# Float64 weight words converted without a clamp, and another written order of the first half of a fused attention and two-MLP kernel

## Chip, cores and metric

The kernel runs on one core of one Trainium2 chip. The metric is the device time of one execution in microseconds (us). A core has TensorE (PE, with its weight loads listed as PEld), VectorE (DVE), ScalarE (ACT), GpSimd (POOL) and SyncE (SP), which here issues all transfers.

## What is computed

Windowed attention with a few global tokens, then two MLPs one after the other. Activations are float32; the weights reach the kernel as float64 words.

```python
# attention: batch 4, heads 8, 512 local and 32 global tokens, head size 64, window 32
s_g  = scale * q_g @ [k_g, k_l].T ;  out_g = sm(s_g) @ [v_g, v_l]
s_l  = [scale * q_l @ k_g.T, where(|i - j| <= 32, scale * q_l @ k_l.T, -1e9)]
out_l = sm(s_l) @ [v_g, v_l]
x = concat(out_g, out_l)                      # 2176 tokens x 512
# first MLP, 512 -> 1024 -> 512
h = x @ w_in ; solu = h * softmax(h)
x = layernorm(solu) * g_ln @ w_out
# second MLP, 512 -> 2048 -> 512
h = x @ w_in2
g = where(h >= 1, h, where(h <= -1, 0, (h + 1) ** 2 / 4))
out = g @ w_out2
```

## The kernel before

Tokens go in 17 tiles of 128. A float32 product is made of three reduced-precision products (high x high, high x low, low x high), so each matrix needs a high and a low part. `conv` makes these from a piece of weights, 128x512 float64 words, which lie in memory as pairs of 32-bit words (`w.low`, `w.high`). Its steps have letters: A takes the magnitude of the high word, C clamps it, B shifts it left by 3, D puts the sign in, F puts in three bits of the low word, m scales by the layernorm gain (second matrix only), H rounds to the high part, L subtracts to get the low part. B, D and F run on VectorE; A and H on ScalarE or VectorE; C and L on GpSimd or VectorE.

The first half of the kernel is written out by hand in `SCRIPT`, a list of tokens that `issue` turns into instructions in that order, on every engine's queue at once. A token is a kind and a number; a trailing `v` picks the other engine for that step. Tokens of the attention of tile n: `q`, `v` load; `S` scores, `M` mask, `R` row maximum (negative), `Rn` scale it, `E` exponentials, `T` transposes, `P` copies of them to SBUF (`PT`), `V` product with the values, `I` reciprocal of the sum, `X` normalize, `XT` transpose back. `G` and `Gc` are the scores of the global tokens and their copy. Of the first MLP: `w` loads a piece, `xh`, `xl` split x, `ha`, `hA`, `hb`, `hB` multiply by `w_in` (each half: high part of x, then low part), `mx` row maximum of h, `ex` exponential, `u` the product h * e * (1/sum), `bn`, `pw`, `nn` layernorm, `t`, `th`, `tl` transpose and split, `y` the second product. `Z` is three products of a zero tile that keep TensorE running.

`psA` (3 banks), `psH` (2 pairs of banks) and `psY` hold products. `psH` is shared: the scores `S` of a tile and the products `h` of a tile take turns in it, so a product waits until the reader of the pair two turns earlier is done. Eight pieces of `w_in` (w0 to w7) must be converted before tile 0's products are complete: w0 to w3 for `ha0`, w4 to w7 for `hb0`.

Behind the script come the remaining tiles (`b1`, `b3`, `b4`, `attention` in the order of `ORDER_1`), and then the second MLP, where a loop over 30 half tiles converts one piece per one or two rounds, clamp included, behind the other work of VectorE (line 177 is the clamp, 175 and 174 are step A, 179 B, 181 D, 183 F, 191 L).

Of the kernel before, what the change touches and what calls it, by code (L numbers as in the profile page):

```python
# [53 lines left out]
F2 H2 Ta0 H1v w3 A3v C3 L1 M1 R1 Rn1 Ea1 Z0 q2 S2 G2 Gc2 Eb1 B3 D3 w0 Pa0 A0v C0 M2 R2 Rn2 Ie0v
Ea2 Z0 q3 S3 B0 F3 H3 L3 G3 Z0 Gc3 D0 Tb0 v0 Pb0 V0 w6 q4 w5 M3 Eb2 F0 L2 H0 qg1 gm0 R3 Rn3v gn0
I0 X0 XT0 A6 C6 B6 D6 Ta1 Pa1 Tb1 Pb1 A5v C5 L0 S4 M4 R4 ge0 B5 gt0 gp0 G4 Gc4 Ie1v I1 Ta2 D5 F5
Ie2 F6 H6v L6 Ea3 Eb3 gc0 v1 q5 H5v L5 xh0 xl0 Rn4v V1 Pa2 Tb2 S5 Ie3v X1 XT1 M5 v2 G5 Gc5v R5
I3 w4 A4v C4 w7 Pb2 V2 I2 X2 A7v Ea4 Eb4 Rn5v XT2 q6 Ta3 Tb3 Pa3 Pb3 B4 C7 B7 S6 G6 Gc6v Ea5 Eb5
Ta4 D7 F7 H7 Tb4 v3 V3 ha0 w10 hA0 Ie4v L7 D4 F4 M6 R6 xh1 H4 Pa4 Pb4 X3 L4 XT3 A10 C10 v4 B10
D10 Rn6v Ie5v Ea6 hb0 hB0 mx0 q7 Eb6 G7 Gc7v V4 I4 X4 S7 Ta5 w11 ex0 ze0 z0 u0 w8 A8 C8 M7 R7  # L60
Rn7 B8 Tb5 Pa5 Pb5 w9 Ta6 Tb6 xl1 ha1 hb1 n0 hB1 Ie6v XT4 w14 xh2 xl2 hA1 bn0v pw0 D8 gi0 F8 F10
v5 V5 I5 Ea7 Eb7 A14 mx1 m8 nn0v ex1 ze1v Pa6 Pb6 ha2 hA2 C14v B14 D14 m10 H10 L10 hb2 gm1 ta0
gn1 ge1 q8 hB2 F14 m14 tha0 vn0 gv0 X5 xh3 xl3 z1 qg2 tb0 u1 XT5 tla0 mx2 go0 w13 thb0v tlb0 H14
v6 H8v A9 C9 ex2 ze2 z2 u2 gt1 gp1 gc1 bn1v pw1 nn1v v7 S8 M8 V6 G8 Gc8 I6 X6 L8 B9 q9 ha3 A11
hA3 tb1 thb1 Tb7 Ie7 D9 F9 m9 L14 ta1 w15 hb3 tlb1 tha1v tla1 H9v R8 Ta7 Pa7v L9 v8 Pb7 bn2v hB3
s0 mx3 A13 C13 Rn8v Ea8 Eb8 qg3 G9 C11v B13 B11 Gc9v pw2 nn2v D11 ya0 F11 XT6 I7 m11 V7 X7 H11v
vn1 A15 C15 B15 ex3 ze3v xh4 z3 S9 M9 u3 R9 L11 Rn9 ta2 tha2v tla2 xh5 xl4 tb2 thb2 tlb2 w12 A12
C12 B12 D12 F12 bn3v pw3 Ya0 yca0 Ta8 Pa8v Ea9 Eb9 m12v xl5 ha4 hA4 Tb8 H12 hb4 hB4 mx4 ex4 ze4v
Ie8 gi1 ha5 hA5 z4 u4 nn3v v9 Pb8 D15 F15 D13 F13 L12 hb5 xh6 q10 G10 Gc10 m13 XT7 S10 M10 Ie9
I9 q11 G11 V8 Gc11 H13 L13 hB5 mx5 tb3 m15 gm2 xh7v H15v L15 bn4v yb0 Yb0 ycb0 pw4 ta3 v10 I8 X8  # L70
R10 Rn10 XT8 nn4v A16v C16 thb3v tlb3 Ea10 gv1 tha3v tla3 s1 A17 s2 A18v go1 C17v Tb9 Eb10 Ie10v
B17 ya1 C18v ta4 tha4 tla4 Ta9 Pa9 Pb9 gn2 ex5 ze5 Ya1 yca1 z5 u5 bn5v pw5 ge2 B16 D16 Ta10 tb4
thb4v tlb4 nn5v V9 X9 q12 ha6 S11 M11 R11 F16 XT9 Pa10 xl7 Rn11 Ea11 xl6 hb6 Tb10 xd0 hB6 hA6
mx6 Pb10v D17 F17 I10 ex6 ze6 z6 Eb11 Ie11v yb1 Yb1 ycb1 B18 u6 xd1 D18 F18 H18 L18 ta5 tha5
tla5 S12 H17v M12 bn6v pw6 xh8v xl8 gt2 v11 gp2 R12 Rn12v ha7 hb7 nn6 q13 tb5 thb5v G12 gc2
# [1207 lines left out]
```

## Time and profile before

| | before |
|---|---|
| time, median of 3 runs | 672.46 us (672.03 to 673.53) |
| the profiled execution: its time | 674.86 us |
| its span, first to last instruction | 672.9 us |
| granted TensorE clock, mean | 0.995 |
| busy: PE, DVE, ACT, POOL | 655.8, 432.7, 371.9, 265.0 us |

The span covers the program's own instructions; the time of the execution is 1.96 us longer. Busy time is an average over stages with different limits, so the rows further down are read by stretch.

### The profile page before, as it was taken

To read this page: it belongs to the slowest core of one execution; us is meant where nothing else is said; L and a number is where in the kernel's file an instruction comes from. 1 tells how busy PE (TensorE), PEld (TensorE's weight loads), DVE (VectorE), ACT (ScalarE), POOL (GpSimd) and SP (SyncE) were. 2 spreads that over 40 slices of the span, in tenths; PEclk is the share of its full clock that TensorE was granted. 3 is DMA by queue.
4 is the path that set the end of the run, shared out by engine and by line. 5 is a ranking of instruction groups with operands and counts; after the bars stand their busy time and mean duration, and the time that the engine had idled before them with its cause. 6 is when DMAs were issued, how large, how long until landed. Compare 5 with 4: busy or idle time off the path is not lost.

```text
span 672.9 us, 15123 instructions
## 1 busy us (share of the span) xinstructions
PE 655.8 (97%) x6088; PEld 576.1 (86%) x6092; DVE 432.7 (64%) x766; ACT 371.9 (55%) x917; POOL 265.0 (39%) x298
## 2 busy tenths in 40 slices
PE   7789999999999999999999999999999999999997
PEld 4467888889899889999999998998888888988986
DVE  5898998785777579754887679455555453333332
ACT  5788886766554244435666555554445466444443
POOL 3354543131112114203444676356766655222321
PEclk9899999999999999999999999999999999999999
DMA  8999654319353604301666342653333465734512
GB/s 337 401 353 362 259 183 174 111 49 334 127 193 102 245 31 125 95 1 32 187 188 188 126 126 63 226 212 126 126 126 127 139 204 194 239 131 157 183 67 80
DMA packets 29686, 113.19 MB, mean 168 GB/s; under 512 B 3376, under 2 KB 3888, under 8 KB 27056
## 3 DMA queue, kind: packets, MB, share of 16 engines
q1 hardware_dynamic: 29616, 112.23, 48.0%
q8 instruction: 48, 0.79, 0.5%
q14 instruction: 22, 0.18, 0.1%
HBM read 87.83 MB, written 24.38 MB: 167 GB/s over the span
## 4 chain that ended last, share of the span: by engine, by line
PE 91%; DVE 5%; issue 1%; ACT 1%; DMA 1%; POOL 0%; DVEq 0%; ACTq 0%; POOLq 0%
PE acc L271 27%; PE h L271 25%; PE h L530 14%; PE yT L271 14%; PE plnT L595 2%; PE o L433 2%; PE S L352 2%; PE pPT L418 2%; PE y L271 1%; DVE nm L141 1%; DVE S L141 1%; PE og L493 1%; DVE xy L141 1%; DVE w L181 1%; PE G L405 1%
## 5 line engine op out<-in xcount | busy, mean ns | idle before, releaser
L271 PE MATMUL acc<-wo,g 128*128 128x512 f32 x816 | 211.3, 393 | 0.0
L271 PEld LDWEIGHTS acc<-wo,g 128*128 128x128 f32 x816 | 149.8, 188 | 23.2
L165 POOL TENSOR_TENSOR g<-xy,g 128x384 fp32r<-128x384 f32 (+1 forms) x65 | 62.8, 973 | 139.9 <-ACT g L150 122.4
L150 ACT ACTIVATE xy<-xy 128x384 f32<-128x384 f32 (+1 forms) x144 | 72.7, 505 | 71.9 <-DVE xy L141 68.8
L530 PE MATMUL h<-win,x 128*128 128x512 f32 x408 | 101.4, 400 | 0.9 <-issue 0.9
L271 PE MATMUL yT<-lnT,wout 128*128 128x256 f32 x768 | 95.2, 283 | 0.0
L271 PEld LDWEIGHTS yT<-lnT,wout 128*128 128x128 f32 x768 | 92.8, 189 | 0.8 <-issue 0.2
L530 PEld LDWEIGHTS h<-win,x 128*128 128x128 f32 x408 | 74.8, 188 | 18.1 <-issue 1.7
L141 DVE TENSOR_TENSOR xy<-h,xy 128x384 f32<-128x384 f32 (+1 forms) x64 | 33.5, 524 | 62.4 <-PE h L271 61.0
L778 POOL TENSOR_TENSOR g<-xy,g 128x192 fp32r<-128x192 f32 x60 | 51.4, 876 | 54.2 <-ACT g L150 46.9
L150 ACT ACTIVATE g<-xy 128x384 fp32r<-128x384 f32 (+1 forms) x96 | 48.0, 500 | 18.7 <-DVE xy L141 16.7
L271 PE MATMUL h<-yT,w2i 128*128 128x384 f32 (+1 forms) x300 | 56.4, 334 | 0.0
L150 ACT ACTIVATE xy<-h 128x384 f32<-128x384 f32 (+1 forms) x64 | 30.0, 468 | 45.9 <-PE h L271 45.9
L271 PE MATMUL h<-yT,S 128*128 128x384 f32 (+1 forms) x288 | 54.8, 325 | 0.0
L271 PEld LDWEIGHTS h<-yT,w2i 128*128 128x128 f32 x300 | 52.5, 188 | 2.3
L141 DVE SCALAR_TENSOR_TENSOR xy<-h,xy 128x384 f32<-128x384 f32 (+1 forms) x48 | 26.2, 545 | 43.8 <-ACT xy L150 43.7
L271 PEld LDWEIGHTS h<-yT,S 128*128 128x128 f32 x288 | 48.8, 188 | 5.6 <-DVE xy L141 1.8
L150 ACT ACTIVATE e<-S,nm 128x128 f32<-128x128 f32 x128 | 45.0, 378 | 8.4 <-DVE nm L141 5.7
L518 POOL TENSOR_TENSOR x<-xy,x 128x512 fp32r<-128x512 f32 x17 | 21.8, 1288 | 41.1 <-ACT x L150 41.0
L572 POOL TENSOR_TENSOR rstd<-rstd,nhalf 128x1 f32<-128x1 f32 x17 | 10.3, 603 | 62.7 <-DVE rstd L141 45.5
L271 PE MATMUL h<-yT,lnT 128*128 128x384 f32 (+1 forms) x180 | 34.1, 334 | 0.1
L141 DVE SCALAR_TENSOR_TENSOR xy<-xy 128x384 f32<-128x384 f32 (+1 forms) x48 | 29.0, 603 | 7.5 <-ACT xy L150 7.3
(145 smaller groups left out, 1059.4 us busy)
## 6 DMA issues: line engine op xcount, KB each, us to landing
vw<-in_vwin_dram SPq DMA_DIRECT2D x16, 1024.0 KB, 5.7
wo<-w2d_o SPq DMA_DIRECT2D x32, 512.0 KB, 3.6
qkT<-in_qk_dram SPq DMA_DIRECT2D x15, 768.0 KB, 7.1
wraw<-in_w2i_dram SPq DMA_DIRECT2D x16, 512.0 KB, 4.9
wraw<-in_w2o_dram SPq DMA_DIRECT2D x16, 512.0 KB, 4.3
w2d_o<-wo SPq DMA_DIRECT2D x16, 512.0 KB, 5.2
...
```

The lines of the kernel that those rows point to most:

```text
L141: self.last = getattr(nc.vector, name)(*args, **kw)
L150: vec.act = nc.scalar.activation(**kw)
L165: eng.tensor_tensor(out=lo, in0=src, in1=hi.bitcast(F32), op=ALU.subtract)
L271: mm(out=dst, lhsT=pairs[i][0][x], rhs=pairs[i][1][y], start=start and j == 0, stop=stop and j == 3 * n - 1, **kw)
L352: mm(out=S[32 * hp:32 * hp + 32, par, ci], lhsT=qT[r, hp, ci], rhs=kT[r, hp, w:w + 4].rearrange("p c d -> p (c d)"), start=True, stop=True)
L418: nc.tensor.transpose(ps[:, hp], eT[t][:, HP * par + hp], ident)
L433: mm(out=o[rows, ci, par], lhsT=PT[t][:, par, ci, rows], rhs=w[:, ci, D * h:D * h + D], start=True, stop=True)
L518: eng.tensor_tensor(out=xT[t][1], in0=x[:, :, n:n + P], in1=xT[t][0].bitcast(F32), op=ALU.subtract)
L530: mm(out=hps[t][:, half], lhsT=x[i][:, k], rhs=win[j][:, k, sl], start=not lo and j == 0 and k == 0, stop=lo and k == KD - 1)
L572: nc.gpsimd.tensor_tensor(sts[t].rstd, sts[t].rstd, nhalf, ALU.pow)
L595: nc.tensor.transpose(ps[:, k], ln[t][:, P * c:P * c + P], ident)
L778: eng.tensor_tensor(out=out, in0=x, in1=y, op=ALU.subtract)
```

## The change

The clamp (step C, 19 tokens in the script, and once per piece in the two loops behind it) is gone. Step A is now a product of the high word, read as a float32, with 2^-112: it brings the exponent into float32's place after the shift, and the shift by 3 drops what lay above. B is a shift alone; D takes the sign bit alone. Step A stays on ScalarE (a copy with a scale in place of an absolute value) or, with `v`, on VectorE (a product in place of a bitwise and). C's tokens leave `SCRIPT`, and the whole list stands in another order, with other `v` marks: of the low parts L, six are now on VectorE (before none); of the splits `xh`, seven of nine (before two); of the layernorm's last step `nn`, five of eight (before one).

```diff
 SCRIPT = """
-w1 Z0 A1 C1 B1 D1 Z0 F1 q0 Z0 S0 qg0 G0 Gc0 Z0 w2 Z0 A2 M0 C2 q1 S1 R0 Rn0v Ea0 Eb0 B2 G1 Gc1 D2
+q0 S0 qg0 Z0 M0 R0 Rn0 G0 Gc0v Z0 w0 A0 Ea0 Eb0 B0 D0 F0 H0v q1 S1 M1 R1 G1 L0 Gc1 w2 A2 B2 D2
...
-WORD_LO = 2.0 ** -15
-WORD_HI = 2.0 ** 17 - 2.0 ** -7
+REBIAS = 2.0 ** -112
+SIGN = -1 << 31
...
-            if eng is nc.vector:
-                return nc.vector.tensor_scalar(w.t, w.high, 0x7FFFFFFF, None, ALU.bitwise_and)
-            return nc.scalar.activation(out=w.tf, in_=w.high.bitcast(F32), func=AF.Abs)
-        if step == "C":
-            return clamp.tensor_scalar(w.tf, w.tf, WORD_HI, WORD_LO, ALU.min, ALU.max)
+            if eng is not None:
+                return eng.tensor_scalar(w.tf, w.high.bitcast(F32), REBIAS, None, ALU.mult)
+            return nc.scalar.activation(out=w.tf, in_=w.high.bitcast(F32), func=AF.Copy, scale=REBIAS)
         if step == "B":
-            return nc.vector.tensor_scalar(w.t, w.t, 3, 0x3FFFFFF8, ALU.logical_shift_left, ALU.bitwise_and)
+            return nc.vector.tensor_scalar(w.t, w.t, 3, None, ALU.logical_shift_left)
         if step == "D":
-            return nc.vector.scalar_tensor_tensor(out=w.t, in0=w.high, scalar=-0x40000000, in1=w.t, op0=ALU.bitwise_and, op1=ALU.bitwise_or)
+            return nc.vector.scalar_tensor_tensor(out=w.t, in0=w.high, scalar=SIGN, in1=w.t, op0=ALU.bitwise_and, op1=ALU.bitwise_or)
...
                 if piece_now:
-                    conv("C", piece_now)
+                    conv("B", piece_now)
...
                 if piece_now:
-                    for step in "BDF":
+                    for step in "DF":
                         conv(step, piece_now)
```

The start of VectorE's queue, before (`w_151` is the piece w1, `w_232` is w2; `S` the scores of a tile, `nm` its row maximum):

```order
L179 TENSOR_SCALAR w_151<-w_151 128x512
L181 SCALAR_TENSOR_TENSOR w_151<-xy_89,w_151 128x512
L183 SCALAR_TENSOR_TENSOR w_151<-xy_89,w_151 128x512
L141 TENSOR_TENSOR S<-S,masks 128x8x2x32
L141 MEMSET S 128x2x32
L141 TENSOR_REDUCE nm<-S 128x8
L179 TENSOR_SCALAR w_232<-w_232 128x512
L181 SCALAR_TENSOR_TENSOR w_232<-xy_89,w_232 128x512
L183 SCALAR_TENSOR_TENSOR w_232<-xy_89,w_232 128x512
```

The same place now (`w_218` is the piece w0; `Sg<-G` copies the global scores):

```order
L140 TENSOR_TENSOR S<-S,masks 128x8x2x32
L140 MEMSET S 128x2x32
L140 TENSOR_REDUCE nm<-S 128x8
L140 TENSOR_SCALAR nm<-nm 128x8
L140 COPY Sg<-G 128x160 x2
L176 TENSOR_SCALAR w_218<-w_218 128x512
L178 SCALAR_TENSOR_TENSOR w_218<-xy_89,w_218 128x512
L180 SCALAR_TENSOR_TENSOR w_218<-xy_89,w_218 128x512
L184 CAST win_133<-w_218 128x512
```

The queue now begins with the mask of tile 0 and no longer with a piece. In both orders seven score tiles and nine shifts stand ahead of the first row maximum over h. VectorE's rows up to that maximum otherwise differ by these: now one more D or F (18 for 17), two copies of `PT` (0), one split of x (1 for 0), one reciprocal (5 for 4) and one sum with epsilon (2 for 1), and two steps A fewer (3 for 5). From there to the third maximum over h come further ones: one D or F more, two splits of x, one low part of `wout`, one cast of `wout`, and five small ones, against two copies of `G` fewer.

TensorE's queue where the first products by `w_in` begin (`win_133` is the high part of `w_in`, `win_134` the low), before:

```order
L352 MATMUL S<-qkT 32x128 x32
L405 MATMUL G<-qkT,qkg 32x128 x8
L418 MATMUL pPT<-ident,e 128x128 x8
L433 MATMUL o<-vw,PT 32x64 x32
L530 MATMUL h<-win_133,x 128x512 x4
L530 MATMUL h<-win_134,x 128x512 x4
L530 MATMUL h<-win_133,x 128x512 x8
```

and now:

```order
L415 MATMUL pPT<-ident,e 128x128 x8
L349 MATMUL S<-qkT 32x128 x32
L430 MATMUL o<-vw,PT 32x64 x32
L527 MATMUL h<-win_133,x 128x512 x4
L527 MATMUL h<-win_134,x 128x512 x4
L402 MATMUL G<-qkT,qkg 32x128 x8
L527 MATMUL h<-win_133,x 128x512 x8
```

The same work stands ahead of `ha0` in both (the scores of tiles 0 to 6, the transposes of 0 to 4, the value products of 0 to 3); the scores `G7` now lie inside tile 0's products, before they came behind them.

ScalarE's queue behind the first row maximum over h (`e_1085`, now `e_1046`, is tile 0's exponential and layernorm; `e,rs<-S` are the exponentials of tile 7's scores; `e_1218`, now `e_1280`, is tile 1's), before:

```order
L150 ACTIVATE junk,rstd<-e_1085,nmu 128x1024
L150 ACTIVATE rstd<-rstd 128x1
L150 ACTIVATE e,rs<-S,nm 128x128 x8
L175 ACTIVATE w_1211<-wraw 128x512
L150 ACTIVATE nmu<-nmu,rstd 128x1
L150 ACTIVATE e_1085<-e_1085,nmu,rstd 128x1024
L150 ACTIVATE e_1218,s_1219<-h,nm_1213 128x1024
```

and now:

```order
L149 ACTIVATE junk,rstd<-e_1046,nmu 128x1024
L149 ACTIVATE rstd<-rstd 128x1
L149 ACTIVATE PT<-pPT 128x512 x2
L149 ACTIVATE nmu<-nmu,rstd 128x1
L149 ACTIVATE e_1046<-e_1046,nmu,rstd 128x1024
L149 ACTIVATE e,rs<-S,nm 128x128 x4
L174 ACTIVATE w_1209<-xy_90 128x512
L149 ACTIVATE e,rs<-S,nm 128x128 x4
```

The exponentials of tile 7 moved behind tile 0's layernorm. They free the `psH` pair that `ha2` takes.

## Rows read from the trace of the kernel before

**Rows 1.** The page: busy time and share of the span of each engine.
```profile
PE 655.8 (97%) x6088; PEld 576.1 (86%) x6092; DVE 432.7 (64%) x766; ACT 371.9 (55%) x917; POOL 265.0 (39%) x298
```

**Rows 2.** Windows: stretch, length, busy us (count) by engine, clock, DMA share, GB/s.
```profile
0.00:20.00 20.00, 14.91 (x338) 8.51 (x346) 12.74 (x24) 11.50 (x49) 5.91 (x21) 0.91 0.89 349
20.00:40.00 20.00, 15.01 (x448) 10.54 (x431) 17.15 (x31) 16.24 (x68) 9.12 (x8) 0.91 0.99 381
40.00:60.00 20.00, 17.96 (x353) 13.87 (x352) 19.10 (x41) 18.58 (x75) 8.68 (x10) 1.00 0.97 377
```

**Rows 3.** Timeline of TensorE: start, length, work, [idle before and what ended it].
```profile
45.18 5.85 PE L530 MATMUL h<-win,x 128*128 128x512 f32 x24
50.96 0.45 PE L405 MATMUL G<-qkT,qkg 64*32 64x128 f32 x16
...
58.05 4.23 PE L530 MATMUL h<-win,x 128*128 128x512 f32 x17 [0.86 <-issue]
...
63.24 4.92 PE L530 MATMUL h<-win,x 128*128 128x512 f32 x20
...
69.46 0.65 PE L493 MATMUL og<-vn,PgT 128*32 128x64 f32 x32
...
71.12 0.66 PE L595 MATMUL plnT<-ident,e 128*128 128x128 f32 x4
```

**Rows 4.** Timeline of VectorE, first 64 us: start, length, work, [idle before].
```profile
5.98 0.43 DVE L179 TENSOR_SCALAR w<-w 128x512 int32<-128x512 int32 x1 [4.87 <-POOL w L177]
...
16.11 0.43 DVE L174 TENSOR_SCALAR w<-xy 128x512 int32<-128x512 int32 x1 [0.57 <-DMA xy<-in_w1i_dram]
...
28.68 0.43 DVE L179 TENSOR_SCALAR w<-w 128x512 int32<-128x512 int32 x1 [0.77 <-POOL w L177]
...
35.40 1.52 DVE L187 CAST win<-w 128x512 fp32r<-128x512 f32 x1
...
51.07 1.23 DVE L141 TENSOR_REDUCE nm<-h 128x1 f32<-128x1024 f32 x1 [0.26 <-PE h L530]
...
62.32 1.23 DVE L141 TENSOR_REDUCE nm<-h 128x1 f32<-128x1024 f32 x1 [1.87 <-PE h L530]
```

**Rows 5.** Groups of VectorE, first 62 us: count | busy, mean ns | idle before.
```profile
L183 DVE SCALAR_TENSOR_TENSOR w<-xy,w 128x512 int32<-128x512 int32 x7 | 4.7, 686 | 0.1
...
L187 DVE CAST win<-w 128x512 fp32r<-128x512 f32 x3 | 2.4, 788 | 0.0
...
L174 DVE TENSOR_SCALAR w<-xy 128x512 int32<-128x512 int32 x3 | 1.2, 406 | 0.6 <-DMA xy<-in_w1i_dram 0.6
```

**Rows 6.** Groups of VectorE, first 230 us.
```profile
L141 DVE COPY PT<-pPT 128x512 f32<-128x512 f32 x3 | 2.0, 680 | 0.0
...
L141 DVE CAST x<-xy 128x512 fp32r<-128x512 f32 x2 | 0.9, 470 | 0.0
```

**Rows 7.** Timeline of GpSimd, around 35 us.
```profile
35.23 1.41 POOL L191 TENSOR_TENSOR win<-w,win 128x512 fp32r<-128x512 f32 x1 [3.06 <-DVE win L187]
```

**Rows 8.** Groups of GpSimd, first 62 us.
```profile
L177 POOL TENSOR_SCALAR w<-w 128x512 f32<-128x512 f32 x10 | 6.1, 613 | 22.7 <-ACT w L175 9.2 <-DVE w L174 8.6 <-PE pPT L418 4.8
```

**Rows 9.** Timeline of ScalarE, 50 to 62 us.
```profile
52.33 1.11 ACT L150 ACTIVATE e<-h,nm 128x1024 f32<-128x1024 f32 x1 [0.30 <-DVE nm L141]
...
61.10 1.24 ACT L150 ACTIVATE e<-e,nmu,rstd 128x1024 f32<-128x1024 f32 x1
```

**Rows 10.** Groups of ScalarE, first 62 us.
```profile
L150 ACT ACTIVATE e<-S,nm 128x128 f32<-128x128 f32 x64 | 22.5, 380 | 2.0 <-DVE xn L141 1.4 <-DVE nm L141 0.6
...
L175 ACT ACTIVATE w<-xy 128x512 f32<-128x512 f32 x4 | 2.7, 669 | 2.3 <-DMA xy<-in_w1i_dram 2.3
```

**Rows 11.** The chain, 390 to 430 us: start, length, work.
```profile
398.97 2.12 PE h L271 x12
...
413.21 0.74 DVE w L177
...
419.97 2.38 PE h L271 x12
```

More of the change, by code (lines that the diff above doesn't have):

```diff
@@ L52 @@
 SCRIPT = """
-w1 Z0 A1 C1 B1 D1 Z0 F1 q0 Z0 S0 qg0 G0 Gc0 Z0 w2 Z0 A2 M0 C2 q1 S1 R0 Rn0v Ea0 Eb0 B2 G1 Gc1 D2
[L54 to L75, printed above, removed]
@@ new lines @@
+gp0 gc0 S4 M4 R4 I0 Pb0 V0 X0 B4 G4 Gc4 D4 L5 Ie1v XT0 A1 B1 D1 F1 I1 Rn3v Ta1 Ea3 Rn4v Tb1 A7v
+B7 Z0 Pa1 Pb1 Z0 D7 Eb3 v1 V1 H1 X1 F7 xh0v xl0 Ta2 Tb2 Pa2 Pb2 G5 Gc5 F4 H4v L4 Ie3v I3 XT1 q6
+G6 S5 M5 R5 v2 Gc6 V2 Ea4 Tb3 Eb4 X2 XT2 Ta3 Pa3v Rn5v Z0 n0 v3 Tb4 L1 w6 A6v B6 Pb3 Ta4 q7 Ea5
+Eb5 S6 V3 Ie4 D6 w11 H7 ha0 L7 I4 M6 R6 Pa4 Pb4 Ie5v Rn6v F6 H6 G7 Gc7 X3 XT3 w10 A10 hA0 B10
+D10 F10 L6 hb0 hB0 mx0 Ea6 Eb6 v4 V4 Ta5 X4 XT4 xh1 ex0 ze0 z0 xh2v u0 Pa5 Tb5 Pb5 v5 w9 A9 B9
+m10 S7 I5 Ta6 D9 H10 L10v M7 Tb6 R7 v6 Rn7 V5 bn0v w12 gm1 Ie6 I6 xl1 ha1 hA1 X5 xl2 hb1 hB1 Pa6
@@ new lines @@
+mx1 pw0 Pb6 nn0v Ea7 A11 ta0 vn0 Eb7 gv0 F9 gi0 go0 tha0 tla0 m9 w8 A8v B8 v7 D8 ex1 ze1 w13 ha2
+hb2 hB2 gn1 XT5 qg2 z1 xh3v ge1 gt1 gp1 H9v tb0 thb0 B11 w14 D11 F11 m11 H11 Ta7 gc1 u1 bn1v L11
+pw1 F8 m8 hA2 xl3 mx2 ex2 ze2v L9v tlb0 q8 A13 V6 X6 z2 u2 ha3 Pa7 hb3 G8 Ie7 Gc8v B13 D13 S8
+H8v L8 nn1v ta1 tha1 tla1 M8 R8 w15 tb1 thb1 I7 tlb1 xh4 Tb7 Pb7 v9 hB3 bn2v pw2 XT6 nn2 hA3 mx3
+V7 Rn8v F13 Ea8 Eb8 A15v X7 ex3 ze3 z3 ya0 u3 tb2 q9 Ya0 G9 thb2v tlb2 m13 H13 S9 Ie8 A14v M9 R9
+Gc9 L13 qg3 ha4 A12 B12 ta2 tha2 Rn9 Ea9 v8 B15 xl4 D15 F15 hb4 tla2 hB4 Ta8 Tb8 Eb9 xh5v Pa8
@@ L165, in split, with conv @@
         eng.tensor_tensor(out=lo, in0=src, in1=hi.bitcast(F32), op=ALU.subtract)
-    def conv(step, w, eng=nc.gpsimd, clamp=nc.vector):
+    def conv(step, w, eng=nc.gpsimd):
         if step == "A":
@@ L199, in convert @@
         for w in ws:
-            first = conv("A", w)
+            first = conv("A", w, None)
             if vec.gate == "both" and vec.act is not None:
@@ L203, in convert @@
         for w in ws:
-            first = conv("C", w)
+            first = conv("B", w)
             if vec.gate and vec.last is not None:
                 behind(first, vec.last)
-        for step in "BDF":
+        for step in "DF":
             for w in ws:
@@ L943, in piece @@
                 pieces[i] = pieces[i]() if i in pieces else stash_word()
-            conv(step, pieces[i], eng, eng)
+            conv(step, pieces[i], eng)
         def issue(c):
-            kind, i, v = re.fullmatch("([A-Za-z]+)([0-9]+)(v?)", c).groups()
+            kind, i, v = re.fullmatch("([A-Za-z]+)([0-9]+)([vp]?)", c).groups()
             i = int(i)
-            eng = nc.vector if v else nc.gpsimd
+            eng = nc.vector if v == "v" else nc.gpsimd
             b, half = divmod(i, 2)
-            if kind in tuple("ACBDFmHL"):
-                piece(kind, i, eng)
+            if kind in tuple("ABDFmHL"):
+                piece(kind, i, None if kind == "A" and not v else eng)
             elif kind == "n":
@@ L1158 @@
                     piece_next = word(make(), raw, scale)
-                    conv("A", piece_next)
+                    conv("A", piece_next, None)
                 if piece_now:
-                    for step in "BDF":
+                    for step in "DF":
                         conv(step, piece_now)
```

15 lines of the change are left out of this document (12 added, 3 removed).

## Prediction

> **What bounds the kernel now.** I read the page first, then the windows, then the timelines of the engines in the stretch that the windows single out, and last the chain. The page gives TensorE 655.8 us busy [rows 1] of a span of 672.9, so 17.1 us are idle in all. The windows say where: 5.1, 5.0 and 2.0 us in the first three stretches of 20 us [rows 2], 12.1 us together; the other 613 us of the span share 5.0. So only the first 60 us have room. In them VectorE is the engine to watch (17.2 and 19.1 us busy in the second and third stretch), and the transfers run at 0.89 to 0.99 of the DMA engines [rows 2].
>
> TensorE's timeline shows the turn at 45.18 us, where the first products by `w_in` start. From there to 80 us it is full but for one wait, 0.86 us before 58.05, put down to "issue": no other engine was awaited [rows 3]. So the time of the kernel is when these products start and whether they keep going, plus work that is the same in both kernels.
>
> VectorE's timeline shows what delays them. Its first useful work starts at 5.98 us, behind a load, step A and a clamp on GpSimd. It is idle six times from there to the first row maximum over h at 51.07 us: 0.57 (first), 0.46, 0.87, 0.91, 0.77 and 0.26 us (last), 3.84 us in all [rows 4]. A cast there takes 1.52 us [rows 4], where three of its group take 2.4 us [rows 5], so the other two 0.42 each: 1.1 us were lost. The waste of this stretch is then 4.94 us of 45.09.
>
> **The removed clamps.** In the first 62 us ten clamps run on GpSimd, 613 ns each [rows 8]. GpSimd is mostly idle there, so the 6.1 us are worth nothing by themselves; what counts is the delay that one puts into a piece. VectorE waited for one only twice: at the start, and 0.77 us before 28.68 us [rows 4]. The start is no gain. Before, it waited for a load of 0.52 MB, step A (0.67) and the clamp (0.61). Now it waits for tile 0's scores, whose load of 0.79 MB is first in the queue: 0.27 MB more are 0.8 us at 349 GB/s [rows 2], and the products of the scores stand in place of the other 0.5. I take the same 6.0 us. The 0.77 goes.
>
> The slow cast ran while GpSimd subtracted from 35.23 to 36.64 us [rows 7], and ended 0.28 us after that. [...]
>
> **The other form of A, B and D.** Same engine, shape and count of passes. The trace shows no product with a constant in place of A; its neighbours are the and, 406 ns on VectorE [rows 5], and the absolute value, 669 ns on ScalarE [rows 10]. I take the same. Were it a slower form, the row to bound it is a pass with two inputs, 686 ns [rows 5]: 0.28 us on each of three steps ahead of the first maximum, 0.8 us. I see no reason for it and leave it in the range only.
>
> **The new order on VectorE.** By the rows of the order, VectorE has more to do ahead of the first maximum over h: one D or F (0.69), two copies of `PT` (2 x 0.68), one split of x (0.47), a reciprocal and a sum over eight columns (taken as 0.2 each), less two steps A (2 x 0.41): 2.1 us more [rows 5, 6]. The four clamps with `v` were all later. So the first maximum comes at 51.07 - 4.94 + 2.1 = 48.2 us plus the waste of the new order. With none it is 2.9 us earlier, with the same 4.94 it is 2.1 us later: those are the bounds. For the value I strike the 0.77 (clamp), the 0.57 (a load which the new order has no VectorE step waiting for so early), and 0.46 and 0.87 (waits for early scores, whose loads now stand further ahead). What stays is 0.91 + 0.26 + 1.10 = 2.3 us. First maximum: 50.5 us, 0.6 earlier.
>
> **Behind it.** TensorE ends tile 0's products at 51.03 us and starts `ha2` at 63.24, 12.2 us later; `G7` (0.4) and the "issue" wait (0.86) are in this [rows 3]. Now `G7` is done by the time of the maximum, so the rest takes 12.2 - 0.4 = 11.8 us with that wait, 10.9 without. The maximum 0.6 us earlier and `G7` make 1.0 us of gain, the "issue" wait 0 or 0.86 more: TensorE has the same count of instructions, and where the wait falls can't be read. I take half and write **1.4 us** for the opening as a whole. Bounds: without waste 2.9 + 0.4 + 0.9 = 4.2 us won, with the old waste 2.1 - 0.4 = 1.7 us lost.
>
> This holds if ScalarE keeps up. `ha2` takes the `psH` pair of tile 7's scores, whose exponentials now stand behind tile 0's layernorm. From the maximum's end ScalarE has three passes over 1024 columns (1.11 to 1.24 each, 3.6), seven over 512 (two steps A, one H, four copies, at 0.67 as A: 4.7), eight exponentials at 22.5/64 = 0.35 (2.8) and a few tiny ones (0.4): 11.5 us [rows 9, 10]. So the pair is free at 50.5 + 1.2 + 11.5 = 63.2 us. TensorE arrives at 50.5 + 10.9 = 61.4 plus a transpose (0.4) and the global values (1.7, from 69.46 to 71.12 [rows 3]), which now stand ahead of `ha2`: 63.5. Costed at nothing; with the cover gone each further us of ScalarE is one of the kernel's.
>
> Still later VectorE has 3.6 us more between the first and the third maximum over h (one D or F 0.69, two splits 0.94, a low part 0.69, a cast 0.42, small ones), where it idled 1.87 us before [rows 4]. I price it from the end of tile 1's products on: if the waste stays at my 2.3 us, the 5.7 us more less 4.5 us of waste saved (2.6 ahead of the first maximum, 1.87 behind it) put the third maximum 1.2 us later than before, by the clock, while TensorE is 1.4 us earlier. What waits for it are the scores of tile 8, which take the `psH` pair of tile 2's products. They stood ahead of `ha3`, and now stand behind `ha3`, `hb3` and `G8`; these are 16 products at 5.85/24 us and one `G`, 4.1 us [rows 3]. 4.1 is more than 2.6, so nothing shows, with 1.5 us to spare.
>
> **The second MLP.** One place there hangs on VectorE: a group of twelve products takes 2.12 us, but 2.38 at 419.97 us, and the chain to it passes through a clamp, 0.74 us [rows 11]. Without the clamp the 0.26 us go: **0.3 us** won, bounds 0 and 0.3. The other clamps there lie beside a full TensorE.
>
> **Sum.** 1.4 + 0.3 = 1.7 us. The profiled execution took 674.86 us, 1.96 over its span of 672.9; it would take 673.2. It is 2.40 us above the median of the three runs (672.46), so the forecast there is 670.8 us.
>
> **Rivals.** (1) *The gain is used up.* The clamps were hidden, and the new order trades one wait for another: with a waste of 3.3 us the first maximum is 0.4 late, `G7` and half the "issue" wait give 0.8 back, and with the 0.3 some 0.7 us are won: 671.8 us, no change that can be told. For it: VectorE's work grew, and ScalarE was 18.6 us of 20 busy [rows 2]. Against it: two of the waits have lost their cause.
>
> (2) *VectorE becomes the bound at tile 8's scores*, slower. The place is the `psH` pair of tile 2's products. Were the waste as before, 4.94 + 1.87, the third maximum would be 5.7 us later by the clock; the new place of the scores covers 4.1 of it. From tile 2 on the kernel would be 1.6 us late, and as the layernorm of tile 2 feeds the first `y`, which has no such cover, it can be the 2.6 or more that separate it from mine: I price it at 2.5 us late, with the 0.3 won 2.2 more, 674.7. It decides from a waste of 3.8 us on (1.5 over mine) and costs net time from about 5.2 on. For it: 5.7 us more on an engine with at most 6.8 to spare. Against it: the products of tile 3 and of `w_out` are long pieces of TensorE that need nothing of tile 8.
>
> (3) *The new order packs without waste*: 4.2 + 0.3 us won, 668.0 us. For it: 4.94 us of waste is what there is to save, and each clamp that delayed VectorE unseen in its idle time would add to it. [...] Against it: transfers at 0.97 to 0.99 in the second and third stretch [rows 2] do not get shorter.
>
> **Chances.** A difference of 0.2%, 1.35 us, is about what a measurement of this kernel can tell from none. Forecast (gain of 1.0 to 2.5 us) 0.45, rival (1) 0.27, rival (2) 0.20, rival (3) 0.08. Faster by over 0.2%: four fifths of the forecast's cases, and all of (3), 0.45; slower: most of (2) 0.19; within: the rest, 0.36. The range reaches from near rival (3), 668.4, to short of (2)'s end, 674.3; the likeliest case alone is 670.0 to 671.5.
>
> **What would show it.** In the new trace: VectorE's first mask near 6 us; first maximum over h near 50.5 us, with some 2.3 us of idle and slowed work ahead of it; `ha0` near 44 us, and from there no wait of TensorE over 0.5 us but "issue"; `ha2` near 63.5 to 64.4; the scores of tile 8 without a wait; no group of 2.38 us near 418 us; step A on either engine at its old length. Wrong it would be if VectorE's waste ahead of the first maximum is near 5 us, if A is a slower form, or if TensorE waits for a `psH` pair between 60 and 90 us.

## The result: 0.9% slower, and the profile after

The changed kernel takes **679.27 us** (median of 4 runs, 677.73 to 682.1), the kernel before 673.0 us beside it; the ratio is **1.0089**, 95% interval [1.0067, 1.0112]. Forecast were 670.8 us, with 668.4 to 674.3 as range: wrong in sign and outside the range. The profiled execution took 677.73 us with a span of 676.0, 3.1 us over the span before.

The page after, first part (busy time) and third (transfer queues: packets, MB, share):
```profile
PE 654.0 (97%) x6087; PEld 576.0 (85%) x6092; DVE 422.6 (63%) x747; ACT 365.9 (54%) x906; POOL 244.8 (36%) x275
...
q8 instruction: 48, 0.79, 0.5%
```
VectorE has 10 us less work than in [rows 1], GpSimd 20 us. The second line is the same in both kernels and becomes important below: 48 transfers of 16 KB. TensorE's records are the 6087 + 6092 of the first line and 99 that wait or drain, 12278 in all, 255.8 for each transfer.

The windows after, columns as in [rows 2]:
```profile
0.00:20.00 20.00, 10.69 (x273) 6.78 (x274) 11.52 (x22) 9.61 (x40) 4.78 (x18) 0.91 0.85 297
20.00:40.00 20.00, 15.19 (x433) 10.03 (x437) 18.90 (x37) 16.11 (x64) 3.85 (x3) 1.00 0.97 360
40.00:60.00 20.00, 17.12 (x444) 13.33 (x431) 16.77 (x31) 15.96 (x67) 8.90 (x8) 1.00 0.82 318
```
TensorE does 4.2 us less in the first stretch than in [rows 2], and the transfers move 297 GB/s in place of 349. GpSimd's work in the second stretch fell from 9.12 to 3.85 us: two clamps (1.2 us) left it, and two low parts of weights stand there (2.5 us) where five stood before (6.7 us).

TensorE's timeline after, the lines that answer to the first of [rows 3] and four of the waits ahead of it:
```profile
4.07 2.90 PE L349 MATMUL S<-qkT 64*32 64x128 f32 x64 [4.07 <-DMA qkT<-in_qk_dram]
...
15.46 1.89 PE L349 MATMUL S<-qkT 64*32 64x128 f32 x64 [3.95 <-DMA qkT<-in_qk_dram]
...
30.74 0.53 PE L430 MATMUL o<-vw,PT 128*32 128x64 f32 x20 [0.96 <-issue]
...
48.03 1.10 PE L430 MATMUL o<-vw,PT 128*32 128x64 f32 x64 [1.99 <-DVE S L140]
49.06 2.13 PE L527 MATMUL h<-win,x 128*128 128x512 f32 x8
```
The first products of h start at 49.06 us, 3.9 later than before. The wait of 1.99 us is put down to VectorE's mask, but that mask stands behind this product in the written list, so it can't be what TensorE waits for; what it is comes out below.

VectorE's timeline after, the lines that answer to [rows 4]:
```profile
7.11 0.70 DVE L140 TENSOR_TENSOR S<-S,masks 128x512 f32<-128x512 f32 x1 [5.98 <-PE S L349]
...
17.40 0.70 DVE L140 TENSOR_TENSOR S<-S,masks 128x512 f32<-128x512 f32 x1 [1.03 <-PE S L349]
...
31.32 0.69 DVE L140 TENSOR_TENSOR xn<-o,rs 128x512 f32<-128x512 f32 x1 [0.50 <-PE o L430]
...
39.22 1.40 DVE L184 CAST win<-w 128x512 fp32r<-128x512 f32 x1
...
45.25 0.43 DVE L173 TENSOR_SCALAR w<-wraw 128x512 f32<-128x512 f32 x1 [0.18 <-DMA wraw<-in_w1i_dram]
...
52.65 0.43 DVE L176 TENSOR_SCALAR w<-w 128x512 int32<-128x512 int32 x1 [1.67 <-ACT w L174]
...
55.51 1.23 DVE L140 TENSOR_REDUCE nm<-h 128x1 f32<-128x1024 f32 x1 [0.98 <-PE h L527]
```
The first row maximum over h is at 55.51 us, 4.4 later than before. Read as the forecast read [rows 4]: five idle times, 1.03 + 0.50 + 0.18 + 1.67 + 0.98 = 4.36 us, and a cast slowed by 1.40 - 0.43 = 0.97, make 5.33 us of waste in 48.40. Three of the five stand ahead of the same step as one of the old six: tile 2's mask (1.03, was 0.46), the normalizing of tile 0's weighted values (0.50, was 0.91) and the maximum itself (0.98, was 0.26). The 0.18 and the 1.67 are new. The 1.67 is ahead of a piece of `w_out` and costs nothing here: from 49.06 us on TensorE runs without a wait until tile 0's products end, and the maximum starts when they do. `ha2` starts at 68.97 (63.24 before); from 80 to 660 us TensorE is full in both of these profiles (580.0 and 579.6 us of 580).

### The profile page after: what moved, and what is told of

Same layout as the page of the kernel before. It is cut to its first block, busy times and chain, and to the rows that moved or that the text cites. A ratio compares the mean times of both kernels' runs of the same rounds, so it can differ in the third digit from the quotient of the medians.

```text
span 676.0 us, 15054 instructions
## 1 busy us (share of the span) xinstructions
PE 654.0 (97%) x6087; PEld 576.0 (85%) x6092; DVE 422.6 (63%) x747; ACT 365.9 (54%) x906; POOL 244.8 (36%) x275
## 4 chain that ended last, share of the span: by engine, by line
PE 92%; DMA 4%; DVE 2%; ACT 1%; issue 1%; SPq 0%; DVEq 0%
PE acc L268 28%; PE h L268 26%; PE yT L268 14%; PE h L527 14%; PE plnT L592 2%; PE o L430 2%; PE S L349 2%; DMA qkT<-in_qk_dram 1%; PE pPT L415 1%; DMA vn<-in_vloc_dram 1%; DMA wraw<-in_w1i_dram 1%; PE y L268 1%; PE og L490 1%; PE G L402 1%; PE pg L470 0%
## 5 line engine op out<-in xcount | busy, mean ns | idle before, releaser
L775 POOL TENSOR_TENSOR g<-xy,g 128x192 fp32r<-128x192 f32 x60 | 48.5, 828 | 57.2 <-ACT g L149 53.1
```

Of the source, the lines that this page charges most:

```text
L775: eng.tensor_tensor(out=out, in0=x, in1=y, op=ALU.subtract)
```

## Experiments

Theories. **A**: late loads (queries, weights, values) hold TensorE up. **F**: blocks of TensorE's own instructions come late, behind the loads, and TensorE stops at the edge of a block (called a stop here; the profile puts most of them down to "issue"). **C**: TensorE's clock. **V**: VectorE's greater work. **B**: the new form of the passes. **L**: the loss lies behind the opening. A bold number is the median of all runs of a kernel, with its ratio to the kernel before (672.9 to 673.8 us beside them) and the 95% interval; the changed kernel's own is 1.0089.

### Form and order apart

e1: the list of before, its 19 clamp tokens dropped, with the new passes.
```diff
-w1 Z0 A1 C1 B1 D1 Z0 F1 q0 Z0 S0 qg0 G0 Gc0 Z0 w2 Z0 A2 M0 C2 q1 S1
+w1 Z0 A1 B1 D1 Z0 F1 q0 Z0 S0 qg0 G0 Gc0 Z0 w2 Z0 A2 M0 q1 S1
```


> The list of before without its clamps, with the new form of A, B and D: the change without its new order. Theory A (the new order makes the loss: TensorE waits for late transfers at the start and VectorE has more to do ahead of the first row maximum over h): at or a little below before, 671.5 to 673.0 us, first maximum over h at 50 to 51 us. Rival B (the new form of the passes is slower, or the loss of the clamp's delay upsets the rest): over 675 us, with steps A, B or D longer than before.

Measured: **674.69 us**, 1.001 [0.9996, 1.0024]; first maximum at 50.59 us. The time lies between the two ranges (A to 673.0, B from 675 on), the maximum where A had it. Removing the clamps is worth nothing here. VectorE starts at 5.05 us, 0.9 sooner, and its wait for the clamp before 28.68 [rows 4] is gone, but its timeline has this:
```profile
26.66 0.69 DVE L140 TENSOR_TENSOR xn<-o,rs 128x512 f32<-128x512 f32 x1 [1.65 <-PE o L430]
```
The wait for tile 0's weighted values was 0.91 and is 1.65 us: VectorE, ahead by the clamp, waits for TensorE instead. And a wait of TensorE appears at 266.93 us, 1.05 long, which comes back below ("the second place").

e2: the old passes, a clamp on GpSimd right behind each A, in the new order.
```diff
-q0 S0 qg0 Z0 M0 R0 Rn0 G0 Gc0v Z0 w0 A0 Ea0 Eb0 B0
+q0 S0 qg0 Z0 M0 R0 Rn0 G0 Gc0v Z0 w0 A0 C0 Ea0 Eb0 B0
```


> The old form with its clamps, all on GpSimd right behind each A, in the new order: the change without its new form. Theory A: as slow as the changed kernel, 678 to 682 us, first products of h near 49 us. Rival B: back near before, under 675 us.

Measured: **684.06 us**, 1.0148 [1.0123, 1.0174]; first products of h at 51.86. Its waits on VectorE in the first 80 us (total, times, longest):
```profile
DVE w L179 <- POOL w L177: 5.2, 6, 1.7
```
That is more than A had (678 to 682 us, products near 49), but B falls: the new order loses with the old form too (1.0148), and with the new form, which takes 4 us off that loss, it still loses (1.0089). What a clamp is worth depends on the order around it: nothing in the old, 4 us in the new, where VectorE waits for one ahead of six steps.

### The opening or what follows it

e12: the list of before up to the first `ha0`, then the new one; e14: the reverse.
```diff
-S6 V3 Ie4 D6 w11 H7 ha0 L7 I4 M6 R6
+S6 V3 Ie4 D6 w11 H7 F6 H6v L6 ha0 w10 hA0 L7 M6 R6
```
(e14 at the seam, old tokens behind H7.)

> The new form, with the list of before up to the first product of h and the new list behind it. All theories of the opening (A, C, F): the time is that of before, 672.5 to 675 us, first maximum over h at 50 to 52 us (five passes of piece 4's conversion and its split now come behind the start of the products). Rival L (the new list loses behind the opening, where the third maximum over h came 6.7 us late and the time between 62 and 80 us grew): 676 us or more.

> The new list up to the first product of h, and behind it the list of before without clamps: the mirror of the run with the old opening (675.5 us). If the loss lies in the opening: 678 us or more, the first maximum over h at 54 to 56 us. Rival L (it lies behind): 676 us or less.

Measured: e12 **675.49 us** (1.0039 [1.0024, 1.0055]), between the two forecasts; e14 **679.29 us** (1.0081 [1.0055, 1.0108]), first maximum at 56.28. The new opening alone gives the changed kernel's time within its interval; the new list behind an old opening is 1.9 us over e1 by the ratios, part of it at the seam, since e12's first maximum came at 54.41 and not at 50 to 52, behind the passes moved there. The larger part of the loss is in the opening; L falls as its main place.

### One wait at a time: clock, loads, VectorE

Six runs each take one suspect away.
```diff
 e3  -q0 S0 qg0 Z0 M0 R0 Rn0 G0 Gc0v Z0 w0
     +q0 Z0 Z0 S0 qg0 M0 R0 Rn0 G0 Gc0v w0
 e4  -S0 qg0 Z0 M0 R0 Rn0 G0 Gc0v Z0
     +S0 qg0 G0 Z0 M0 R0 Rn0 Gc0v Z0
 e8  w5 ahead of q2, w6 behind it; S5 ahead of G5
 e15 -H3 q5 A4 ... w7 gt0 Tb0 w1 ... Eb3 v1 V1
     +H3 w1 v1 q5 A4 ... w7 gt0 Tb0 ... Eb3 V1
 e13 -Pa0v ... xh0v ... Pa3v
     +Pa0 ... xh0 ... Pa3
 e9  e3, and Z0 ahead of S1 (x4), S2 (x2), G3, Pb0, V3
```


> The changed kernel, with the six products with zeros that stand behind tile 0's scores put ahead of them (VectorE's and the load queue's order stay). TensorE then works from about 1.2 us on while the first load is under way. Theory C (the start costs time through TensorE's clock: tile 0's scores ran at the lower of the two levels, 2.90 us in place of 1.16): first mask 1.1 to 1.7 us earlier, near 5.5 to 6 us, the third load of queries and keys issued as much earlier, the mean granted clock steady, and 2 to 4 us won on the changed kernel, 675 to 677 us. Rival A alone (transfers and VectorE's work bound the opening whatever the clock): under 0.7 us won.

> The changed kernel, with tile 0's global scores right behind its scores on TensorE and the three products with zeros behind them (nothing moved on VectorE or in the load queue). Tile 0's queries and keys are then read about 1.1 us sooner, so that the load for tile 2, which takes their place and whose wait of 4.1 us is TensorE's longest, is issued near 8.0 in place of 9.15 us. Theory A: the wait ending at 15.46 us ends 1.1 us earlier and the time falls by 0.5 to 1.1 us. Theory C: scores of tile 0 as slow as now, so no more than that; under C alone no gain.

> The changed kernel with the loads of weight pieces 5 and 6 put ahead (5 ahead of the load for tile 2, whose wait leaves the transfers idle; 6 in 5's place), and tile 5's scores ahead of the global scores that wait for tile 6's load. Theory A: tile 5's scores start near 37.5 in place of 39.0 us, VectorE no longer waits for piece 6, and 1 to 2.5 us are won, 677 to 678 us. Theory F: TensorE stops at the same instructions and gains under 0.7 us.

> The changed kernel with the loads of weight piece 1 and of tile 1's values issued ahead of that for tile 5 (whose wait they stood behind): near 20 in place of 24 us, landing 2 to 4 us sooner. Theory A: tile 1's weighted values and piece 1's conversion start up to 1 us sooner, and up to 1 us is won. Theory F: 1.5 MB more then stand ahead of the block of instructions that TensorE asks for near 23 us, so that the stop before instruction 961 (0.96 us, ending at 30.74) grows by 1 us or more and ends after 32 us; the time grows by up to 2 us.

> The changed kernel with three copies and casts of the opening (two copies of the transposed exponentials, the high part of tile 0's x) on ScalarE in place of VectorE, which takes 1.7 us of VectorE's work away ahead of the first maximum over h. Rival V (VectorE's greater work bounds the opening): first maximum over h 1.2 to 1.7 us earlier, near 54 us, and the time as much less, 677.5 us. Theory F or A (TensorE's blocks of instructions and the loads): first products of h within 0.7 us of 49.06, the time within 1 us of 679.3.

> The changed kernel with TensorE's idle time of the opening filled: 30 more products with zeros (0.21 us each), ahead of the scores of tiles 1 and 2, of tile 3's global scores and of the weighted values of tiles 0 and 3, and the first six ahead of tile 0's scores. Theory C (TensorE's clock, which falls after its idle time, makes the loss and its spread): the mean granted clock at 0.996 or more, as before, the times within 1 us of each other, and 3 us or more won, 676 us or less. Theory A or F (late loads and late blocks of instructions): TensorE starts the products of h no sooner than 48 us, and the time stays at 677 to 681 us, whatever the clock.

Measured: e3 **679.04** (1.0075), e4 **679.30** (1.0066), e8 **680.06** (1.0101), e15 **678.92** (1.0077), e13 **679.36** (1.0087), e9 **678.40 us** (1.0073). The intervals (0.0018 to 0.0029 to each side) all hold 1.0089, so no gain can be told; the largest, e4's, would be 1.5 us. So C's forecasts for e3 and e9 (675 to 677 us, 676 or less) and A's for e8 (677 to 678 us) missed. The edits did what they say at their own places: in e3 the first mask is at 6.13 and tile 2's scores start at 13.58 in place of 15.46, in e4 at 13.73. Not in e8, where tile 5's scores start at 39.70 and not near 37.5. And the gains of e3 and e4 are gone by 31 us, at one place, inside tile 0's weighted values: TensorE's "issue" wait there is 2.96 us in e3, 2.81 in e4, 2.13 in e8, 2.34 in e15 (0.96 in the first profile after). That it ends at 30.94 and 31.00 us in e3 and e4 and at 30.74 without the edit, however early TensorE comes, speaks for F. In e15 it ends at 32.66, as F said, but the time did not grow: F's sign at that stop was right, its price for the kernel not borne out.

In e13 VectorE, with 1.7 us less to do, waits longer:
```profile
22.79 0.43 DVE L176 TENSOR_SCALAR w<-w 128x512 int32<-128x512 int32 x1 [2.51 <-ACT w L174]
...
47.15 0.43 DVE L173 TENSOR_SCALAR w<-wraw 128x512 f32<-128x512 f32 x1 [1.19 <-DMA wraw<-in_w1i_dram]
```
Its first products start at 50.82 and the first maximum is at 57.27, later than V (near 54) and F or A (within 0.7 of 49.06 for the products) had them. V alone falls. On C: e9 brought the granted clock to 0.997 (median of its executions; 0.9915 in the changed kernel's, 0.996 before), and the time is 1.1 of 6.0 us less by the ratios, within the noise, with times that still spread over 5 us. My expectation for e3 spoke of the lower clock at tile 0's scores. The first profiles of both kernels show two levels, 1.00 and 0.50, and others only in windows over a change; in the one after, it is 0.50 from 16 to 19 us, behind the wait of 3.95 us, but the window at tile 0's scores grants 1.00, so their 2.90 us (1.91 with six products ahead) are not shown to be the clock.

### Where TensorE stops, and for what

e5 and e6 put tiny products into a wait, and so move every later instruction to another place in its block; e11 does it to e1; e16 takes 24 instructions out of e1.
```diff
+    def pad(n):
+        ps = psY.tile([P, 512], F32, tag="Y", name="Z")
+        for _ in range(n):
+            mm(out=ps[:, :32], lhsT=zero[:, :P], rhs=zero[:, :32], start=True, stop=True)
...
-q2 S2 M2
+q2 Z32 S2 M2
```
(e6: Z64. e16: without four of the tokens Z0 ahead of S3.)

> The changed kernel with 32 more tiny products with zeros (64 instructions more in TensorE's queue) ahead of tile 2's scores, where TensorE waits 3.9 us anyway. Theory F (TensorE's instructions come by transfers of 16 KB, 256 instructions each, which queue behind the loads; TensorE stops at every 256th instruction when the next block is late): the stop inside the first products of the weighted values, now before instruction 961, comes 64 instructions earlier in the program (near its 12th product in place of the 44th), and the stop ahead of tile 3's weighted values, now before instruction 1729, moves into tile 6's scores; each ends 1.3 to 1.6 us after such a transfer. The time moves by up to 2 us either way. Theory A (late loads of queries, values and weights): the stops stay where they are in the program, and the time stays or grows by what the added products take.

> As the run before with 64 tiny products, 128 instructions. Theory F: the first stop lies inside tile 4's scores, the other one ahead of tile 6's scores, where TensorE comes from slower transposes. Theory A: as with 32, no stop moves.

> The list of before without its clamps (the run with the new form alone) with 32 tiny products with zeros ahead of tile 2's scores. Theory F: its stops, which end at 21.27, 34.10 and 39.10 us in the global scores and the weighted values, move 64 instructions ahead in the program; the time moves by up to 2 us either way from 674.7. Theory A: they stay, and the time stays within 0.7 us.

> The list of before without clamps and without twelve products with zeros (24 instructions) ahead of tile 0's global scores to tile 3's scores. Theory F: the stops near 21.3, 34.1 and 39.1 us come 24 instructions later in the program, and shrink by up to 1.5 us in all: 673 to 674.5 us, if TensorE's clock holds. Without F: the time stays at 674.7 or, where the clock falls for want of these products, grows by 1 to 3 us.

Measured: e5 **679.83**, e6 **684.71** (1.017 [1.0153, 1.0187]), e11 **680.34** (1.0106 [1.0083, 1.0129]), e16 **676.66 us** (1.0054 [1.0036, 1.0073]). 32 tiny products cost e1's kernel 6.5 us by the ratios and the changed one 0.5; 64 cost the changed one 5.5. F had up to 2 us either way. TensorE's "issue" waits in e1:
```profile
21.27 0.67 PE L402 MATMUL G<-qkT,qkg 64*32 64x128 f32 x11 [1.85 <-issue]
...
34.10 0.41 PE L430 MATMUL o<-vw,PT 128*32 128x64 f32 x10 [0.91 <-issue]
...
39.10 0.65 PE L430 MATMUL o<-vw,PT 128*32 128x64 f32 x31 [0.92 <-issue]
```
and in e11, the same list with 64 instructions more:
```profile
20.97 0.55 PE L355 MATMUL S<-qkT 64*32 64x128 f32 x22 [2.03 <-issue]
...
33.26 0.86 PE L436 MATMUL o<-vw,PT 128*32 128x64 f32 x42 [1.15 <-issue]
...
41.89 0.31 PE L355 MATMUL S<-qkT 64*32 64x128 f32 x4 [1.01 <-issue]
56.56 0.66 PE L355 MATMUL S<-qkT 64*32 64x128 f32 x10 [3.77 <-issue]
```
The first stop moved from the global scores (11 products left) into the scores ahead of them, the second from 10 products before the end of the weighted values to 42: 32 products, each a load of weights and a product, 64 instructions. A new stop of 3.77 us came into tile 7's scores, and there the time is lost: the first products of h start at 44.52 us (44.71 in e1), and behind that stop e11 runs 5.3 to 5.4 us later than e1 to its end. So the stop costs more than its length: TensorE stood until 56.56, from 57 to 59 us the granted clock is 0.50, and 16 transposes take 3.28 us (2.00 in e1). In e6 the two stops named in advance are gone, and others are there:
```profile
36.15 1.44 PE L274 MATMUL Z<-zero 128*128 128x512 bf16 x3 [2.58 <-issue]
...
53.25 0.26 PE L436 MATMUL o<-vw,PT 128*32 128x64 f32 x1 [3.68 <-issue]
```
Behind the second of these, too, the clock is 0.50 (53 to 55 us), and the first eight products of h take 3.39 us in place of 2.13. F named the rule rightly and the places in e5 and e6 badly: where a block comes in time there is no stop (in the changed kernel's first profile the one of instruction 1217 landed at 33.58 us, and TensorE came to it at 36.5 without one). In e5 the one before instruction 961 is simply gone, the first products of h start at 47.67, and the gain is lost by a stop of 1.00 us in tile 7's scores and by the second place below. Counted through the trace (a few records are missing, so within 8), the stops of all profiles lie at instructions 705, 961, 1217 and so on, every 256. Some of them, with the 16 KB transfer that ended last (TensorE stood: from the start of its last instruction to that of the next):
```
kernel        instr  TensorE entered   its transfer     TensorE stood
                     the block before
e18 (before)    705      15.22         18.82 - 19.90    19.20 - 21.32
e18 (before)   1217      27.77         31.35 - 32.44    31.66 - 33.75
after           961      23.13         28.30 - 29.34    29.56 - 30.74
after          1729      40.95         45.59 - 46.55    45.77 - 47.92
e17 (after)     961      24.32         30.56 - 31.53    29.80 - 32.86
e11            2241      50.35         54.00 - 55.09    52.52 - 56.56
e6             1985      47.40         50.91 - 51.89    49.35 - 53.25
```
TensorE goes on 1.3 to 1.5 us after the transfer has ended. The wait of 1.99 us that was put down to VectorE is the fourth line. e16 has its stops 24 instructions later, as F says, but they grew (3.60 us at 41.76) and its clock was 0.986 (median of its executions): with both at once it decides nothing, and F's 673 to 674.5 us missed.

The table has stops of the kernel before as well. In its second profile (e18) these stand ahead of the first products of h:
```profile
21.32 0.44 PE L405 MATMUL G<-qkT,qkg 64*32 64x128 f32 x11 [1.85 <-issue]
...
27.76 0.66 PE L352 MATMUL S<-qkT 64*32 64x128 f32 x27 [1.34 <-issue]
...
33.75 0.64 PE L433 MATMUL o<-vw,PT 128*32 128x64 f32 x10 [1.88 <-issue]
```
They are 5.1 us, and 2.5 in its first profile (1.36 at 21.81, 1.17 at 34.58); in the changed kernel they are 3.0 (0.96 and 1.99) and 2.9. So their sum does not tell the two kernels apart. And e5, which has none ahead of its first products, starts these at 47.67, still 2.5 us later than before's first profile and 3.1 later than its second. The runs show what a stop is and where it can fall; that stops make the larger part of the loss is not shown.

e7 leaves out loads, e10 is e7 with e9's products.
```diff
     def load_vw(t):
+        if t in (2, 3):
+            vw[t] = vw[t - 2]
+            return
         vw[t] = ab.tile([P, 4, DM], F32, tag="vw", name="vw")
+        if t < 2:
+            nc.gpsimd.memset(vw[t], 0.0)
+            return
```


> The changed kernel without the loads of the local values of tiles 0 to 3 (their tiles hold zeros from GpSimd; 4 of the 18 MB that land in the first 50 us are left out). Theory F: with less traffic the blocks of instructions come sooner after they are asked for (1 to 3 us in place of 4 to 6), no stop of TensorE over 0.5 us at every 256th instruction, first products of h by 45 us or earlier, 3 us or more won, 675 us or less. Rival V (VectorE's greater work is the bound of the opening): VectorE has the same work, so first maximum over h at 53 us or later, and under 2 us won.

> The same products with zeros, without the loads of the local values of tiles 0 to 3 (as in the run that left these out, whose profiled execution was 4.9 us faster than its other executions). If the clock is what sets those apart (theory C): all executions at 673 to 675.5 us and the clock at 0.996 or more. If it is not: the same spread, 674.6 to 680.4 us.

Measured: e7's profiled execution took 674.64 us (span 672.8, that of before), with the first products of h at 45.86. Its VectorE, every idle time over 0.2 us up to the first maximum:
```profile
27.81 0.70 DVE L140 TENSOR_TENSOR S<-S,masks 128x512 f32<-128x512 f32 x1 [0.42 <-PE S L355]
...
49.80 0.73 DVE L176 TENSOR_SCALAR w<-w 128x512 int32<-128x512 int32 x1 [0.25 <-ACT w L174]
...
52.32 1.23 DVE L140 TENSOR_REDUCE nm<-h 128x1 f32<-128x1024 f32 x1 [0.33 <-PE h L533]
```
1.00 us idle in place of 4.36, and blocks that come in time: in e10 four in a row start 0.55 to 0.66 us after TensorE entered the block before, where the table has 3.5 to 6.2. In three of these four waits the DMA engines are 0.10 to 0.40 busy; the blocks ahead of and behind the four, with the engines full, wait 4.3 and 3.2 us. So in this run most of the early blocks go with little traffic and the late ones with full engines. But these runs take away late loads together with late blocks, so they do not part A from F. And the other executions of e7 took 678.9 to 680.4 us, at a clock of 0.989 to 0.992 against 0.997 in the profiled one, so the median (**679.49**) shows no gain: F's 675 or less missed, and so did V's first maximum at 53 or later. e10, whose clock stayed at 0.996 to 0.997 in all but one, took 676.05 to 677.64 (**676.98**; the other 680.04), more than C's 673 to 675.5. By the ratios (e10 1.0059 [1.0034, 1.0083], e7 1.0081, e9 1.0073) traffic and clock together are worth some 2.0 us of 6.0, which is not clear of the noise, and neither alone more than 1.1.

### Both kernels once more

> The changed kernel as it is, profiled once more. If its usual 679.3 us are the opening and a second place: first products of h at 48.4 to 50.8 us, and a wait of TensorE of about 1.04 us for VectorE near 271 us, which the first profile lacks; 679 to 680.5 us. If the second place is not part of it: no such wait, and the time above 678.5 us only with the first products of h later than 50 us.

> The kernel before as it is, profiled once more: 672 to 675 us, first products of h at 44.5 to 46 us, first maximum at 50.4 to 52 us. The wait of about 1.04 us near 267 us, which the run with the new form alone showed, may be there or not; with it the time is 1.5 us or so longer.

Measured: **680.22** (1.0098) and **673.11 us** (1.0000); both as expected. The changed kernel's second profile, VectorE:
```profile
7.17 0.70 DVE L140 TENSOR_TENSOR S<-S,masks 128x512 f32<-128x512 f32 x1 [6.04 <-PE S L349]
...
17.66 0.70 DVE L140 TENSOR_TENSOR S<-S,masks 128x512 f32<-128x512 f32 x1 [1.23 <-PE S L349]
...
29.23 0.70 DVE L140 TENSOR_TENSOR S<-S,masks 128x512 f32<-128x512 f32 x1 [0.36 <-PE S L349]
...
33.77 0.69 DVE L140 TENSOR_TENSOR xn<-o,rs 128x512 f32<-128x512 f32 x1 [2.27 <-PE o L430]
...
40.51 0.69 DVE L140 TENSOR_TENSOR xn<-o,rs 128x512 f32<-128x512 f32 x1 [1.02 <-PE o L430]
...
57.02 1.23 DVE L140 TENSOR_REDUCE nm<-h 128x1 f32<-128x1024 f32 x1 [0.35 <-PE h L527]
```
With 0.24 us at 54.48 and 0.96 of a slow cast the waste is 6.43 us. TensorE, the stop that causes the 2.27, and a second place:
```profile
32.87 0.85 PE L430 MATMUL o<-vw,PT 128*32 128x64 f32 x20 [2.85 <-issue]
...
273.07 2.17 PE L268 MATMUL yT<-lnT,wout 128*128 128x256 f32 x16 [1.04 <-DVE lnT L140]
```
The span is 678.8 us against 671.4 of before's second profile, whose VectorE began at 5.84 and came to the first maximum at 50.42 with a waste of 4.03 (five idle times, 2.95, and 1.08 of a slow cast). The 7.4 us between the two: 6.6 stand at the first maximum (start 1.3, work 2.9, waste 2.4), of which 6.35 are left at 250 us, 1.4 come between 250 and 281 us, and 0.4 come back behind. The first profile after lacked the second place, and its stop in tile 0's weighted values was short; it is the fastest execution of this kernel's first four. The second place belongs to the form, not to the order: the wait of 1.04 to 1.05 us is in 14 of the 17 profiles without clamps, e1's among them, and in none of the three with clamps (both of before, e2).

## Why the prediction was wrong

**What bounds the kernel.** Right on where there is room (the first 60 us). That the rest is the same holds for the first profile after, not for the second place (1.4 us). I took VectorE as the engine to watch, and put TensorE's own instructions and the transfers down as given. The "issue" wait, of which I wrote that where it falls can't be read, falls at every 256th instruction whose block is late, and there are up to five in an opening (e11).

**The new order on VectorE: the step that failed.** It said "What stays is 0.91 + 0.26 + 1.10 = 2.3 us. First maximum: 50.5 us". Measured was 55.51: start 1.13 us later, work 43.07 in place of 42.25 (0.8), waste 5.33 in place of 2.3 (3.0), 5.0 us in all. In the second profile it is 57.02, with 1.2, 1.2 and 4.1. My own sign of being wrong, a waste near 5 us, is there. Of the six waits that the forecast read, these are the three that [rows 4] does not show:
```profile
16.99 0.70 DVE L141 TENSOR_TENSOR S<-S,masks 128x512 f32<-128x512 f32 x1 [0.46 <-PE S L352]
...
22.96 1.29 DVE L141 TENSOR_REDUCE gnm<-Sg 128x2 f32<-128x1088 f32 x1 [0.87 <-ACT Sg L150]
...
26.46 0.69 DVE L141 TENSOR_TENSOR xn<-o,rs 128x512 f32<-128x512 f32 x1 [0.91 <-PE o L433]
```
What I kept (0.91, 0.26 and the cast's 1.10) came in the first profile as 0.50, 0.98 and 0.97, 2.45 us for 2.3. What failed is the striking. The 0.46, for tile 2's scores, I struck because their load "now stands further ahead"; it came back as 1.03, as TensorE itself waited 3.95 us for that load, which was issued at 9.15 us (before at 8.12), once tile 0's global scores had been made. The 0.87 I read as a wait of the same kind; by its line it was one for ScalarE's copy of the global scores. And I added no wait that the new order makes: 1.67 and 0.18 are new. Under this lies a wrong path: I took the maximum as VectorE's work and waste, but it came when TensorE's products ended, 6.4 us after they had started, and with 1.7 us less work on VectorE (e13) it came no sooner. `ha0` was forecast near 44 us and started at 49.06 and 50.55; TensorE's own way there, its loads, stops and slower products, is not in the sum. In e7 the waste is 1.96 us, near the 2.3, but of other parts (0.42, 0.25, 0.33 and a cast), and the maximum is still at 52.32: the agreement is luck. The bounds failed too: "with the same 4.94" isn't the worst, since waste can grow.

**The start.** "I take the same 6.0 us" was 7.11. The load was there at 4.07, earlier than assumed; tile 0's scores took 2.90 us, and I had allowed 0.5 for them. With six products ahead of them (e3) 1.0 us of it comes back, and is lost at the stop.

**The removed clamps.** The 0.77 went, and VectorE waited for TensorE instead (e1): worth nothing in the old order. Not foreseen was that passes without clamps meet GpSimd's subtractions at the end of the first MLP, 1.4 us in e17; the wait of TensorE that goes with it is in 14 of the 17 profiles without clamps, and the forecast has no term for it.

**The other form.** Right: step A takes 0.43 us on VectorE (45.25, above) and 0.66 to 0.69 on ScalarE, as before.

**Behind it.** `ha2` was forecast at 63.2 to 64.4 and started at 68.97, 13.5 us behind the first maximum where I had 13.0; the 5.0 us of lateness were handed on. No wait over 0.5 us but at the stops, and tile 8's scores without one, both as written.

**The second MLP.** Right. The group of 2.38 us [rows 11] is gone from the chain after, where its like take:
```profile
398.27 2.10 PE h L268 x12
402.45 2.10 PE h L268 x12
```
The changed kernel's lateness falls there from 3.48 to 3.14 us in the first pair of profiles and from 7.77 to 7.44 in the second: the 0.3 was won.

**Rivals.** (2) had the right sign and a wrong place: nothing waits for tile 8's `psH` pair, and its 674.7 us was still 4.6 short. (1) and (3) are out. A rival in which TensorE is late for reasons of its own was missing.

**What stays open.** How the loss of the opening divides between stops, loads, VectorE's 2.9 us of work and the clock: they seem to take each other's place, since removing one showed nothing. The experiments show that the new order loses, and mostly in the opening; which part of it does is not shown. Nor is why the clock is lower in most executions of the new order (the falls behind two long stops, above, are part of such an answer). No version beat the kernel before; e1 is level with it.
